# Attention and a dense mixture of experts on one core: the last v scale by TensorE, and the second halves of the weight splits by ScalarE and VectorE

## The chip, the core and the metric

The kernel runs on one core of one Trainium2 chip. The metric is the device time of one execution in microseconds (us). Engine names as in the profile: PE is TensorE's matrix multiplication and PEld its weight load, DVE is VectorE, ACT is ScalarE, POOL is GpSimd, SP is SyncE, which here only issues DMA. L12 is line 12 of the kernel.

## The reference

Causal attention with a decay, for 4 batches of 8 heads (S = 576 positions, D = 64), and behind it a mixture of 4 experts in which every expert runs on every token:

```python
scores = scale * q @ k.T + (cum[i] - cum[j]);  causal mask;  attn = softmax(scores)
x = (attn @ v)  ->  tokens 2304 x 512
p = domain_probs / (domain_probs.sum(-1, keepdims=True) + 1e-09)
for e in range(4):
    h = np.maximum(x @ w1[e], 0.0)          # 512 -> 1024
    out += p[:, e:e + 1] * (h @ w2[e])      # 1024 -> 512
```

Inputs and output are float32.

## The kernel before

**Numbers as pairs.** Most products run in f16 at float32 quality: a number is scaled by a power of two and written as a high part (`hi`, `wh`, `gh`) and the f16 of the rest (`lo`, `wl`, `gl`), and a product is the sum of high times high, high times low and low times high. A split therefore has two steps: ScalarE writes the scaled number as f16, and another engine takes that from the scaled number. The scale of a tensor is a power of two near its largest magnitude, so it needs a maximum over all 128 partitions.

**Order of work.** Attention comes in two halves of the queries (`JOBS`): in the first half the heads' keys are 256 long, in the second up to 576. The expert layers come in groups (an expert's weights in two halves each, `GROUPS`) of four units of 128 x 1024, a unit holding 512 columns of the first layer (`k == 0`) and 512 of the second (`k == 1`). Until about 85 us the start runs, with the first four groups on float32 pairs; from about 85 to 206 us runs what is here called the first sweep, the groups of steps 4 to 7 on the first tokens, while the later heads of the first half of attention are computed; then the heads of the second half with more groups until about 590 us; then a part in which the sums of products are formed in another way, to the end. The program's text gives the steps of heads (`head_steps`, with `bounds[n]` as extra work at head n), and a scheduler puts the instructions of all engines in an order by its own plan of durations. Each engine then carries out its list strictly in that order, and so does SP with the DMAs.

**Weight units.** `w_split` (L1020 to L1056) splits a unit that was loaded as float32 (`wr`, loaded at L989). There are 32 such units: 16 in the first sweep, 8 around 325 to 365 us and 8 around 480 to 545 us. For the first-layer half, ScalarE writes `wh` (L1043) and VectorE `wl` (L1044, `scalar_tensor_tensor`). For the second-layer half, the number is first scaled in place (first sweep: ScalarE, L1033; later: GpSimd, L1035), ScalarE casts it (L1038), and GpSimd subtracts (L1039). L1053 stores some of the pairs in DRAM for later.

**The v scale.** The scale of v for the second half of attention is global over the batch. `v_scale` (L390 to L430) comes in two parts, `top` at `bounds[30]` and `finish` at `bounds[31]`. `top` reduces over the free axis (L401), has SP write the column of 128 maxima to DRAM (L402, tile `dv`) and read it back, broadcast to all partitions (L403, `tops`); `finish` reduces along the free axis (L408) and forms the power of two and its reciprocal (L409 to L421), into column B of `vsc` and `xun`. These are used by the splits of v in the second half of attention (`prep_v`, L572 and L573) and by `weigh` (L442, GpSimd), which makes the factors `scg` of the sums L1142. The other scales (of weights, `topw`; of v per batch, `topx`) go through `power` (L200 to L241), with PE moving the maxima: a transpose (L206), a reduction and three small steps on VectorE (L209 to L220), a tiny matmul with ones that broadcasts (L227), and `finish` on VectorE (L236, L239).

**Who uses what, around it.** L1077 is the first layer (`l` for gate, its weights `wh`, `wl`), ScalarE (L1090, `gh`) and VectorE (L1091, `gl`) make the hidden pair, L1113 is the second layer, and VectorE's L1142 weights the result into `acc` and so frees the PSUM tile for the next chunk's L1113. L638 are the scores, VectorE's L652 adds the mask and finds the maximum `nm`, L749 splits the probabilities (`z`), and SP's L761 transposes them by DMA into `pt`.

Of the kernel before, what the change touches and what calls it, by code (L numbers as in the profile page):

```python
# [8 lines left out]
F32 = mybir.dt.float32  # L9
F32R = mybir.dt.float32r  # L10
F16 = mybir.dt.float16
I32 = mybir.dt.int32  # L12
AF = mybir.ActivationFunctionType
ALU = mybir.AluOpType
AX = mybir.AxisListType

B, H, S, D = 4, 8, 576, 64
E, DM, FF = 4, 512, 1024
NT = B * S
# [18 lines left out]
SWEEP_1 = 8  # L38
# [42 lines left out]
TINY = 2.0**-26  # L81
EXPONENT = 0x7F800000
# [3 lines left out]
def fused(ctx: ExitStack, tc: tile.TileContext, qk, v, f, probs, w, out):  # L86
    nc = tc.nc
# [4 lines left out]
    const = SB("const", 1)  # L92
# [18 lines left out]
    dr_p = ctx.enter_context(tc.tile_pool(name="dr", bufs=4, space=bass.MemoryType.DRAM))  # L111
# [14 lines left out]
    vmax = const.tile([128, 16], F32, name="vmax")  # L126
    vsc = const.tile([128, 8], F32, name="vsc")
    xsc = const.tile([128, 8], F32, name="xsc")
    xun = const.tile([128, 8], F32, name="xun")
    tops = const.tile([128, 256], F32, name="tops")  # L130
    pr_r = tops[:, : NT // 128 * E].rearrange("p (t e) -> p t e", e=E)
    ones_r = const.tile([4, 128], F32, name="ones_r")
    scg = const.tile([128, 8, NT // 128], F32, name="scg")
    sc0 = const.tile([128, 2, E], F32, name="sc0")
# [109 lines left out]
    known = set()  # L244
# [121 lines left out]
    NV = 6  # L366
# [23 lines left out]
    def v_scale():  # L390

        m = vmax[:, NV : NV + 1]
        d = dr_p.tile([128, 1], F32, tag="dv", name="dv", bufs=1)
        u = vmax[:, NV + 1 : NV + 2]

        def top():
            assert all(("x", b) in known for b in range(B))
            nc.vector.tensor_tensor(
                out=vmax[:, :B], in0=vmax[:, :B], in1=xsc[:, :B], op=ALU.max
            )  # L400
            nc.vector.tensor_reduce(out=m, in_=vmax[:, :NV], op=ALU.max, axis=AX.X)  # L401
            nc.sync.dma_start(out=d, in_=m)  # L402
            nc.sync.dma_start(  # L403
                out=tops[:, :128], in_=d.rearrange("q k -> (q k)").partition_broadcast(128)
            )

        def finish():
            nc.vector.tensor_reduce(out=u, in_=tops[:, :128], op=ALU.max, axis=AX.X)  # L408
            nc.vector.tensor_scalar(out=u, in0=u, scalar1=TINY, scalar2=None, op0=ALU.max)  # L409
            nc.vector.tensor_scalar(  # L410
                out=u.bitcast(I32),
                in0=u.bitcast(I32),
                scalar1=EXPONENT,
                scalar2=None,
                op0=ALU.bitwise_and,
            )
            nc.vector.reciprocal(out=vsc[:, B : B + 1], in_=u)
            nc.vector.tensor_scalar(
                out=xun[:, B : B + 1], in0=u, scalar1=2.0**-2, scalar2=None, op0=ALU.mult
            )  # L420
            nc.vector.tensor_scalar(  # L421
                out=vsc[:, B : B + 1],
                in0=vsc[:, B : B + 1],
                scalar1=2.0**14,
                scalar2=None,
                op0=ALU.mult,
            )
            known.add(("x", B))

        return top, finish  # L430

    weighed = set()

# [487 lines left out]
    bounds = {}  # L921
    for b in range(2, B):
        n = 2 * NPR * b
# [5 lines left out]
        bounds[n - 1] = [(100, parts[3])]  # L929

    parts_v = v_scale()
    bounds[30] = [(50, parts_v[0])]
    bounds[31] = [(50, parts_v[1])]

    def head_steps(n):

# [29 lines left out]
    wh, wl, wraw, loaded = {}, {}, {}, {}  # L966
# [50 lines left out]
    def w_fetch(n):  # L1017
        nc.sync.dma_start(out=w_pair(n), in_=wd[unit(n)])

    def w_split(n):  # L1020
        if n not in RAWS:
            w_fetch(n)
            return
        r = wraw.pop(n)
        g = GROUPS[n // 4][0]
        assert ("w", g) in known
        t = w_pair(n)
        for k in range(2):
            c = slice(512 * k, 512 * k + 512)
            sc = wsc[:, g, k : k + 1]  # L1030
            if k == 1:
                if n // 4 < SWEEP_1:
                    nc.scalar.activation(out=r[:, c], in_=r[:, c], func=AF.Copy, scale=sc)  # L1033
                else:
                    nc.gpsimd.tensor_scalar(  # L1035
                        out=r[:, c], in0=r[:, c], scalar1=sc, scalar2=None, op0=ALU.mult
                    )
                nc.scalar.activation(out=wh[n][:, c], in_=r[:, c], func=AF.Copy)  # L1038
                nc.gpsimd.tensor_tensor(  # L1039
                    out=wl[n][:, c], in0=r[:, c], in1=wh[n][:, c], op=ALU.subtract  # L1040
                )
                continue
            nc.scalar.activation(out=wh[n][:, c], in_=r[:, c], func=AF.Copy, scale=sc)  # L1043
            nc.vector.scalar_tensor_tensor(  # L1044
                out=wl[n][:, c],
                in0=r[:, c],
                scalar=sc,
                in1=wh[n][:, c],
                op0=ALU.mult,
                op1=ALU.subtract,  # L1050
            )
        if (g in KEPT) == (n // 4 < SWEEP_1):
            at_step(step + 1, lambda: nc.sync.dma_start(out=wd[unit(n)], in_=t))  # L1053
        i = RAWS.index(n) + RAW
        if i < len(RAWS):
            w_load(RAWS[i])  # L1056
# [779 lines left out]
```

## Time and profile before

| what | us |
|---|---|
| three runs | 934.6, 935.0, 940.25 |
| median | 935.0 |
| the profiled execution | 933.63 |
| its span in the trace | 931.8 |
| PE busy | 866.4 (93%) |
| DVE busy | 712.5 (76%) |
| ACT busy | 544.4 (58%) |
| POOL busy | 463.9 (50%) |
| mean granted clock of PE, share of full speed | 0.989 |

Busy is the time in which an engine carries out instructions; PE at 93% leaves 65 us in the span without a matmul. In a row of the timeline the columns are the start (us), the duration (us), engine, line, operation, output<-input with shape and type, and in square brackets the idle time of the engine before it with what ended it; xN joins N neighbours of one kind. In a row of waits: the waiting engine and line, <- what it waited for, then total us, how often, and the longest us. In a row of instruction groups: line, engine, operation, output<-input, shape, count | busy us, mean ns of one | idle before us and what ended it.

### The profile page before, as it was taken

To read this page: it belongs to the slowest core of one execution; us is meant where nothing else is said; L and a number is where in the kernel's file an instruction comes from. 1 tells how busy PE (TensorE), PEld (TensorE's weight loads), DVE (VectorE), ACT (ScalarE), POOL (GpSimd) and SP (SyncE) were. 2 spreads that over 40 slices of the span, in tenths; PEclk is the share of its full clock that TensorE was granted. 3 is DMA by queue.
4 is the path that set the end of the run, shared out by engine and by line. 5 is a ranking of instruction groups with operands and counts; after the bars stand their busy time and mean duration, and the time that the engine had idled before them with its cause. 6 is when DMAs were issued, how large, how long until landed. Compare 5 with 4: busy or idle time off the path is not lost.

```text
span 931.8 us, 16630 instructions
## 1 busy us (share of the span) xinstructions
PE 866.4 (93%) x5756; PEld 570.8 (61%) x5756; DVE 712.5 (76%) x1496; ACT 544.4 (58%) x1118; POOL 463.9 (50%) x496
## 2 busy tenths in 40 slices
PE   3698989879999998999999899999998999999998
PEld 2577756446667665676766576654455664666547
DVE  5589799836888899878888867655678747786487
ACT  5766849435676685665767765445655345653350
POOL 3746645344325275325238520384778627885060
PEclk9999999989999999999999999999999999999999
DMA  8667889949999999985897984254322422241003
GB/s 281 197 180 235 232 273 250 256 120 270 252 236 258 228 255 276 238 235 125 209 286 228 299 184 76 56 187 140 114 74 91 159 91 89 70 124 36 24 1 91
DMA packets 167236, 163.64 MB, mean 176 GB/s; under 512 B 105108, under 2 KB 129872, under 8 KB 167152
## 3 DMA queue, kind: packets, MB, share of 16 engines
q1 hardware_dynamic: 167152, 162.58, 62.8%
q8 instruction: 45, 0.74, 0.3%
q14 instruction: 39, 0.32, 0.1%
HBM read 116.78 MB, written 21.64 MB: 149 GB/s over the span
## 4 chain that ended last, share of the span: by engine, by line
PE 48%; POOL 9%; DVE 8%; ACT 6%; issue 3%; DMA 1%; SPq 0%; POOLq 0%; ACTq 0%; DVEq 0%
PE l L1077 13%; PE l L1113 13%; PE y L1348 8%; PE m L1348 8%; PE s L638 4%; POOL s L1408 4%; POOL wt L1245 3%; PE o L848 3%; POOL wu L1245 1%; DVE z L749 1%; DVE rl L1234 1%; ACT wt L1272 1%; DVE acc L1142 1%; DVE h L1383 1%; ACT r L1394 1%
## 5 line engine op out<-in xcount | busy, mean ns | idle before, releaser
L1077 PE MATMUL l<-y,w 128*128 128x256 f16 x1728 | 213.9, 274 | 2.1 <-DVE w L1044 2.1
L1077 PEld LDWEIGHTS <-w 128*128 128x128 f16 x1728 | 162.7, 98 | 43.6 <-issue 7.4
L1113 PE MATMUL l<-w,gh 128*128 128x512 f16 x568 | 173.6, 389 | 9.6 <-DVE acc L1142 9.6
L667 ACT ACTIVATE p<-p,nm 128x576 f32<-128x576 f32 (+2 forms) x160 | 95.7, 599 | 87.2 <-DVE nm L652 74.9
L586 POOL CAST q<-raw 64x320 fp32r<-64x320 f32 (+1 forms) x56 | 27.0, 482 | 193.3 <-issue 88.5
L749 DVE SCALAR_TENSOR_TENSOR z<-p,rs,z 128x384 f16<-128x384 f32 (+5 forms) x176 | 109.5, 645 | 16.6 <-ACT z L748 15.3
L1113 PE MATMUL l<-w,gl 128*128 128x512 f16 x284 | 108.4, 387 | 6.9 <-DVE gl L1091 6.9
L748 ACT ACTIVATE z<-p,rs 128x384 f16<-128x384 f32 (+5 forms) x176 | 88.6, 550 | 31.5 <-issue 17.7
L1142 DVE SCALAR_TENSOR_TENSOR acc<-y,scg,acc 128x256 f32<-128x256 f32 (+1 forms) x164 | 81.2, 516 | 14.9 <-PE y L1348 14.7
L1113 PEld LDWEIGHTS <-gh 128*128 128x128 f16 x568 | 51.5, 99 | 60.2 <-issue 19.3
L638 PE MATMUL s<-hi 128*128 128x384 f32 (+1 forms) x192 | 77.1, 409 | 10.9 <-POOL hi L600 5.8
L652 DVE CUSTOM_DVE_ANT_0 p<-s,mask 128x288 f32<-128x288 f32 (+2 forms) x160 | 74.2, 474 | 16.4 <-PE s L638 16.1
L1348 PE MATMUL m<-rh,bs 128*128 128x512 f16 x256 | 86.4, 379 | 0.2 <-POOL bs L1277 0.2
L594 POOL TENSOR_TENSOR kl<-raw,hi 64x576 fp32r<-64x576 f32 (+1 forms) x56 | 66.2, 1182 | 17.8 <-ACT hi L585 17.1
L1277 POOL TENSOR_TENSOR bs<-wt,bs 128x512 f16<-128x512 f32 x32 | 37.9, 1190 | 73.4 <-ACT bs L1276 73.0
L1091 DVE SCALAR_TENSOR_TENSOR gl<-l,gh 128x512 f16<-128x512 f32 (+1 forms) x80 | 54.7, 684 | 16.3 <-ACT gh L1090 15.6
L1348 PE MATMUL m<-rh,bw 128*128 128x512 f16 x191 | 64.5, 379 | 1.0 <-ACT r L1394 0.9
L585 ACT ACTIVATE hi<-raw 128x896 fp32r<-128x896 f32 (+1 forms) x56 | 45.3, 808 | 34.3 <-DMA raw<-in_qk 13.7
L638 PE MATMUL s<-kl,q 66*128 66x384 f32 (+1 forms) x192 | 61.6, 327 | 0.0
L1348 PEld LDWEIGHTS <-bs 128*128 128x128 f16 x384 | 37.5, 98 | 38.8 <-POOL bs L1277 0.7
L1383 DVE SCALAR_TENSOR_TENSOR h<-s,h 128x512 f16<-128x512 f32 x40 | 46.4, 1165 | 17.8 <-ACT h L1382 17.5
L1348 PEld LDWEIGHTS <-h 128*128 128x128 f16 x480 | 46.9, 98 | 14.8 <-issue 2.6
(389 smaller groups left out, 1889.2 us busy)
## 6 DMA issues: line engine op xcount, KB each, us to landing
wr<-in_w SPq DMA_DIRECT2D x74, 512.0 KB
wd<-w SPq DMA_DIRECT2D x32, 512.0 KB
w<-wd SPq DMA_DIRECT2D x32, 512.0 KB
raw<-in_qk SPq DMA_DIRECT2D x32, 448.0 KB
wp<-in_w SPq DMA_DIRECT2D x32, 256.0 KB
bv<-wd SPq DMA_DIRECT2D x32, 256.0 KB
bw<-wd SPq DMA_DIRECT2D x32, 256.0 KB
raw<-in_qk SPq DMA_DIRECT2D x24, 256.0 KB
```

The lines of the kernel that those rows point to most:

```text
L594: eng.tensor_tensor(out=kl[:64, :wk], in0=r[:64, ko : ko + wk], in1=hi[:64, ko : ko + wk].bitcast(F32), op=ALU.subtract,)
L638: nc.tensor.matmul(out=ps[:, at : at + z - a], lhsT=lhsT, rhs=rhs, start=(m == 0), stop=(m == 1),)
L652: nc.vector.tensor_tensor_reduce(out=pt[:, a:z], in0=ps, in1=mask[:, m0 + a : m0 + z], scale=-0.125, scalar=BIG if n == 0 else nm[:, col : ...
L667: nc.scalar.activation(out=pt[:, :w_], in_=pt[:, :w_], func=AF.Exp, scale=-1.0, bias=self.nmax[hh][:, c : c + 1], accum_out=self.ssum[:, h ...
L748: nc.scalar.activation(out=o[:, 0], in_=x, func=AF.Copy, scale=sc)
L749: nc.vector.scalar_tensor_tensor(out=o[:, 1], in0=x, scalar=sc, in1=o[:, 0], op0=ALU.mult, op1=ALU.subtract)
L1077: nc.tensor.matmul(out=self.l1p[:, fi, :], lhsT=lhsT, rhs=rhs[:, k, :], start=(k == 0 and m == 0), stop=(k == 3 and m == 2),)
L1091: self.last = nc.vector.scalar_tensor_tensor(out=self.gl, in0=self.l1p, scalar=0.0, in1=self.gh.bitcast(F32) if wide else self.gh, op0=ALU ...
L1113: matmul(out=l2[tt], lhsT=lhsT, rhs=rhs, start=(opens and fi == 0 and m == 0), stop=(closes and fi == 1 and m == 2),)
L1142: nc.vector.scalar_tensor_tensor(out=acc[c][:, tt, d0:d1], in0=ps, scalar=sc, in1=acc[c][:, tt, d0:d1], op0=ALU.mult, op1=ALU.add,)
L1348: line.append(nc.tensor.matmul(**args))
L1383: nc.vector.scalar_tensor_tensor(out=t[:, 1], in0=x, scalar=0.0 if relu else 1.0, in1=t[:, 0], op0=op, op1=ALU.subtract,)
```

## The change

`v_scale` no longer goes through DRAM. It is built by `power(1, m, "v", use)` and has three parts at `bounds[29]`, `[30]` and `[31]`: free-axis maximum on VectorE and transpose on PE; VectorE's four small steps and the broadcasting matmul; VectorE's `finish` with the two factors. `tops` shrinks to a tile `pr_t` for the probabilities. In `w_split` the branch for `k == 1` is gone: both halves are split by L1043 on ScalarE and L1044 on VectorE.

```diff
-    tops = const.tile([128, 256], F32, name="tops")
-    pr_r = tops[:, : NT // 128 * E].rearrange("p (t e) -> p t e", e=E)
+    pr_t = const.tile([128, NT // 128 * E], F32, name="pr_t")
+    pr_r = pr_t.rearrange("p (t e) -> p t e", e=E)
     def v_scale():
         m = vmax[:, NV : NV + 1]
-        d = dr_p.tile([128, 1], F32, tag="dv", name="dv", bufs=1)
-        u = vmax[:, NV + 1 : NV + 2]
+
+        def use(u, r):
+            nc.vector.tensor_scalar(
+                out=xun[:, B : B + 1], in0=u, scalar1=2.0**-2, scalar2=None, op0=ALU.mult
+            )
+            nc.vector.tensor_scalar(
+                out=vsc[:, B : B + 1], in0=r, scalar1=2.0**14, scalar2=None, op0=ALU.mult
+            )
+            known.add(("x", B))
...
             nc.vector.tensor_reduce(out=m, in_=vmax[:, :NV], op=ALU.max, axis=AX.X)
-            nc.sync.dma_start(out=d, in_=m)
-            nc.sync.dma_start(
-                out=tops[:, :128], in_=d.rearrange("q k -> (q k)").partition_broadcast(128)
-            )
-
-        def finish():
-            nc.vector.tensor_reduce(out=u, in_=tops[:, :128], op=ALU.max, axis=AX.X)
...
-            known.add(("x", B))
-
-        return top, finish
+
+        across, exponent, finish = power(1, m, "v", use)
+        return lambda: (top(), across()), exponent, finish
...
-    bounds[30] = [(50, parts_v[0])]
-    bounds[31] = [(50, parts_v[1])]
+    for n in range(3):
+        bounds[29 + n] = [(50, parts_v[n])]
...
             sc = wsc[:, g, k : k + 1]
-            if k == 1:
-                if n // 4 < SWEEP_1:
-                    nc.scalar.activation(out=r[:, c], in_=r[:, c], func=AF.Copy, scale=sc)
-                else:
-                    nc.gpsimd.tensor_scalar(
-                        out=r[:, c], in0=r[:, c], scalar1=sc, scalar2=None, op0=ALU.mult
-                    )
-                nc.scalar.activation(out=wh[n][:, c], in_=r[:, c], func=AF.Copy)
-                nc.gpsimd.tensor_tensor(
-                    out=wl[n][:, c], in0=r[:, c], in1=wh[n][:, c], op=ALU.subtract
-                )
-                continue
             nc.scalar.activation(out=wh[n][:, c], in_=r[:, c], func=AF.Copy, scale=sc)
             nc.vector.scalar_tensor_tensor(
```

The scheduler plans anew, so the lists of all engines differ from about 85 to 540 us; behind that they are nearly the same. Three places, with the names as above and numbers of tiles behind them (line numbers of the changed kernel are lower: L1013 is what L1044 was, L1022 is L1053, L970 is L989, L742 is L761, L730 is L749, L1060 is L1091, L1111 is L1142).

SP's list before, where the two small DMAs of the v scale stand, in the second half of the first sweep:

```order
L533 DMA raw_1_0_1_2332<-in_qk 128x512
L558 DMA kl_2_0_0_2458<-ncd 2x256
L402 DMA dv<-vmax 128x1
L403 DMA tops<-dv 128x128
L761 DMA_TRANSPOSE pt_0_0_0_2311<-z_691 128x2x128
L761 DMA_TRANSPOSE pt_0_0_0_2311<-z_691 128x4x128
L989 DMA wr_2422<-in_w 128x1024
L989 DMA wr_2430<-in_w 128x1024
L1053 DMA wd_159<-w_2416 128x2048
L1053 DMA wd_160<-w_2424 128x2048
```

SP's list of the changed kernel at the same place, before the same transposes of `pt_0_0_0`:

```order
L970 DMA wr_2410<-in_w 128x1024
L1022 DMA wd_159<-w_2405 128x2048
L970 DMA wr_2417<-in_w 128x1024
L1022 DMA wd_160<-w_2412 128x2048
L970 DMA wr_2521<-in_w 128x1024
L1022 DMA wd_161<-w_2516 128x2048
L970 DMA wr_2528<-in_w 128x1024
L539 DMA kl_2_0_1_2508<-ncd 2x256
L742 DMA_TRANSPOSE pt_0_0_0_2300<-z_692 128x2x128
L742 DMA_TRANSPOSE pt_0_0_0_2300<-z_692 128x4x128
```

The transposes stood behind the DMA that reads `dv` back; now loads and stores of weight units stand there, and no DMA of the v scale.

VectorE's list before, around the reduction L408 of what came back from DRAM:

```order
L702 TENSOR_SCALAR ss_0_0_2239<-ss_0_0_2239 128x2
L705 RECIPROCAL rs_0_0_2240<-ss_0_0_2239 128x2
L749 SCALAR_TENSOR_TENSOR z_691<-p_0_0_0_0_2236,rs_0_0_2240,z_691 128x128
L408 TENSOR_REDUCE vmax<-tops 128x1
L409 TENSOR_SCALAR vmax<-vmax 128x1
L410 TENSOR_SCALAR vmax<-vmax 128x1
L749 SCALAR_TENSOR_TENSOR z_691<-p_0_0_0_1_2237,rs_0_0_2240,z_691 128x2x128
L417 RECIPROCAL vsc<-vmax 128x1
L418 TENSOR_SCALAR xun<-vmax 128x1
L421 TENSOR_SCALAR vsc<-vsc 128x1
L1142 SCALAR_TENSOR_TENSOR acc_1097<-l_6_6_0_0_0_2381,scg,acc_1097 128x512
L1142 SCALAR_TENSOR_TENSOR acc_1097<-l_6_6_0_0_1_2388,scg,acc_1097 128x512
```

VectorE's list of the changed kernel at the same place (its L408 is the free-axis maximum, L401 before):

```order
L683 TENSOR_SCALAR ss_0_0_2228<-ss_0_0_2228 128x2
L408 TENSOR_REDUCE vmax<-vmax 128x1
L1013 SCALAR_TENSOR_TENSOR w_2405<-wr_1666,wsc,w_2405 128x512
L1013 SCALAR_TENSOR_TENSOR w_2412<-wr_1673,wsc,w_2412 128x512
L686 RECIPROCAL rs_0_0_2229<-ss_0_0_2228 128x2
L1013 SCALAR_TENSOR_TENSOR w_2405<-wr_1666,wsc,w_2405 128x512
L1013 SCALAR_TENSOR_TENSOR w_2412<-wr_1673,wsc,w_2412 128x512
L1013 SCALAR_TENSOR_TENSOR w_2516<-wr_1778,wsc,w_2516 128x512 x2
L1013 SCALAR_TENSOR_TENSOR w_2523<-wr_1785,wsc,w_2523 128x512
L1111 SCALAR_TENSOR_TENSOR acc_1098<-l_6_6_0_0_0_2370,scg,acc_1098 128x512
L1013 SCALAR_TENSOR_TENSOR w_2523<-wr_1785,wsc,w_2523 128x512
L1060 SCALAR_TENSOR_TENSOR gl_6_1_0_2473<-l_6_6_1_0_2422,gh_6_1_0_2472 128x512
```

Ahead of the first `acc` of that chunk stood the reduction that waits for the DMA; now seven splits of weights stand there, an eighth between it and the next `gl`.

VectorE's list of the changed kernel some 50 rows later, where the maxima come back from PE's transpose (`topv`; `uv` is a small tile in SBUF):

```order
L209 TENSOR_REDUCE uv<-topv 1x1
L210 TENSOR_SCALAR uv<-uv 1x1
L213 TENSOR_SCALAR uv<-uv 1x1
L883 SCALAR_TENSOR_TENSOR y_2591<-o_0_0_2578,y_2591 128x256
L220 TENSOR_SCALAR uv<-ident,uv 1x1
L554 SCALAR_TENSOR_TENSOR v_2_0_2615<-vh_1539,vsc,v_2_0_2615 128x4x64
L683 TENSOR_SCALAR ss_2_0_2613<-ss_2_0_2613 128x2
L686 RECIPROCAL rs_2_0_2614<-ss_2_0_2613 128x2
```

Between the four steps of the exponent and their neighbours stands other work; `finish` follows ten rows later (L236, L239 and the two factors in a row).

## Rows read from the trace of the kernel before

**Rows 1.** The page, busy time of the engines (us, share of the span, instructions).
```profile
PE 866.4 (93%) x5756; PEld 570.8 (61%) x5756; DVE 712.5 (76%) x1496; ACT 544.4 (58%) x1118; POOL 463.9 (50%) x496
```
**Rows 2.** Waits of PE over the run.
```profile
PE l L1113 <- DVE acc L1142: 9.6, 4, 6.1
PE l L1113 <- DVE gl L1091: 8.4, 8, 2.3
PE s L638 <- DVE nm L652: 4.5, 2, 4.1
PE topx L227 <- DVE ux L220: 3.7, 3, 1.9
```
**Rows 3.** Timeline, 186 to 202 us, all engines.
```profile
186.32 0.69 DVE L1091 SCALAR_TENSOR_TENSOR gl<-l,gh 128x512 f16<-128x512 f32 x1 [0.28 <-ACT gh L1090]
186.88 0.34 SPq L402 DMA_DIRECT2D dv<-vmax  x1
...
188.48 1.03 PE L1113 MATMUL l<-w,gh 128*128 128x512 f16 x4
...
191.07 2.35 PE L1077 MATMUL l<-y,w 128*128 128x256 f16 x20
...
193.81 0.32 SPq L403 DMA_DIRECT2D tops<-dv  x1
...
194.22 6.40 SPq L761 DMA_TRANSPOSE pt<-z  x2
198.35 0.29 DVE L408 TENSOR_REDUCE vmax<-tops 128x1 f32<-128x128 f32 x1 [10.38 <-DMA tops<-dv]
...
200.40 1.87 PE L1113 MATMUL l<-w,gh 128*128 128x512 f16 x4 [6.07 <-DVE acc L1142]
```
**Rows 4.** Busy time by stretch: us, PE, PEld, DVE, ACT, POOL, clock, DMA share, GB/s.
```profile
118.00:172.00 54.00, 46.27 (x320) 29.65 (x318) 53.90 (x129) 34.34 (x84) 28.79 (x40) 0.97 0.90 266
...
195.00:200.00 5.00, 0.00 (x0) 0.00 (x0) 1.58 (x8) 0.00 (x0) 0.29 (x1) 0.90 0.31 26
200.00:205.00 5.00, 3.82 (x9) 1.12 (x9) 4.30 (x13) 1.47 (x5) 5.00 (x10) 0.50 0.73 166
...
340.00:360.00 20.00, 18.29 (x140) 12.48 (x137) 18.98 (x32) 14.07 (x27) 19.69 (x16) 1.00 0.90 262
```
**Rows 5.** The broadcasting matmuls of `power`, instruction groups of PE, whole run.
```profile
L227 PE MATMUL topw<-uw,ones_r 2*128 2x2 f32 x16 | 3.0, 256 | 0.6 <-DVE uw L220 0.6
```
**Rows 6.** Instructions of L1044: count, shortest, median, longest (ns), first and last start.
```profile
L1044 DVE SCALAR_TENSOR_TENSOR w<-wr,wsc,w x32: 730/750/1951, 106.5 to 526.2; 128x512 f16<-128x512 f32 x32
```
**Rows 7.** Timeline, GpSimd's subtractions and VectorE beside them, first sweep.
```profile
161.04 2.26 POOL L1039 TENSOR_TENSOR w<-wr,w 128x512 f16<-128x512 f32 x2
161.28 2.04 DVE L702 TENSOR_SCALAR ss<-ss 128x2 f32<-128x2 f32 x1
```
**Rows 8.** Instruction groups of DVE by shape, 85 to 206 us.
```profile
L1044 DVE SCALAR_TENSOR_TENSOR w<-wr,wsc,w 128x512 f16<-128x512 f32 x16 | 12.7, 811 | 1.8 <-POOL scg L442 1.0 <-ACT w L1043 0.8
...
L749 DVE SCALAR_TENSOR_TENSOR z<-p,rs,z 128x128 f16<-128x128 f32 x14 | 9.2, 660 | 0.0
```
**Rows 9.** The same, 206 to 280 us, where no unit is split.
```profile
L749 DVE SCALAR_TENSOR_TENSOR z<-p,rs,z 128x128 f16<-128x128 f32 x6 | 2.1, 346 | 0.5 <-ACT z L748 0.5
```
**Rows 10.** Instruction groups of DVE, 325 to 365 us.
```profile
L1044 DVE SCALAR_TENSOR_TENSOR w<-wr,wsc,w 128x512 f16<-128x512 f32 x8 | 8.2, 1031 | 0.0
```
**Rows 11.** Timeline of VectorE, four splits of probabilities at two times.
```profile
354.99 5.59 DVE L749 SCALAR_TENSOR_TENSOR z<-p,rs,z 128x384 f16<-128x384 f32 x4
...
510.13 2.26 DVE L749 SCALAR_TENSOR_TENSOR z<-p,rs,z 128x384 f16<-128x384 f32 x4
```
**Rows 12.** Instruction groups of DVE by shape, 480 to 545 us.
```profile
L1044 DVE SCALAR_TENSOR_TENSOR w<-wr,wsc,w 128x512 f16<-128x512 f32 x8 | 10.8, 1363 | 0.0
```
**Rows 13.** Instruction groups of ACT, 85 to 545 us, splits of weights.
```profile
L1043 ACT ACTIVATE w<-wr,wsc 128x512 f16<-128x512 f32 x32 | 22.5, 711 | 1.8 <-PE s L638 1.2 <-DVE wsc L341 0.4
...
L1038 ACT ACTIVATE w<-wr 128x512 f16<-128x512 f32 x32 | 19.4, 616 | 0.0
```

More of the change, by code (lines that the diff above doesn't have):

```diff
@@ L401, in top @@
             nc.vector.tensor_reduce(out=m, in_=vmax[:, :NV], op=ALU.max, axis=AX.X)
-            nc.sync.dma_start(out=d, in_=m)
-            nc.sync.dma_start(
-                out=tops[:, :128], in_=d.rearrange("q k -> (q k)").partition_broadcast(128)
-            )
-        def finish():
-            nc.vector.tensor_reduce(out=u, in_=tops[:, :128], op=ALU.max, axis=AX.X)
[L409 to L415, printed above, removed]
-            )
-            nc.vector.reciprocal(out=vsc[:, B : B + 1], in_=u)
-            nc.vector.tensor_scalar(
-                out=xun[:, B : B + 1], in0=u, scalar1=2.0**-2, scalar2=None, op0=ALU.mult
-            )
[L421 to L427, printed above, removed]
-            known.add(("x", B))
-        return top, finish
+        across, exponent, finish = power(1, m, "v", use)
+        return lambda: (top(), across()), exponent, finish
     weighed = set()
@@ L1030, in w_split @@
             sc = wsc[:, g, k : k + 1]
-            if k == 1:
-                if n // 4 < SWEEP_1:
-                    nc.scalar.activation(out=r[:, c], in_=r[:, c], func=AF.Copy, scale=sc)
-                else:
-                    nc.gpsimd.tensor_scalar(
-                        out=r[:, c], in0=r[:, c], scalar1=sc, scalar2=None, op0=ALU.mult
-                    )
-                nc.scalar.activation(out=wh[n][:, c], in_=r[:, c], func=AF.Copy)
-                nc.gpsimd.tensor_tensor(
-                    out=wl[n][:, c], in0=r[:, c], in1=wh[n][:, c], op=ALU.subtract
-                )
-                continue
             nc.scalar.activation(out=wh[n][:, c], in_=r[:, c], func=AF.Copy, scale=sc)
```

## The prediction

> **What bounds the kernel now.** I read the page's busy times first: PE works for 866.4 of 931.8 us [rows 1], so a change that adds no work to PE can only win from the 65 us in which PE stands still, and from stretches at a lower clock. Next, the waits of PE: which of them does the change touch? Four rows matter [rows 2]. The longest single wait, 6.1 us, is for an `acc` of VectorE, and VectorE's list shows what it stood behind: the reduction L408, which waits for the v scale to come back from DRAM.
>
> The timeline of that place tells the whole story [rows 3]. SP issues the write of `dv` at 186.88 and can issue the read only at 193.81, 6.9 us later; VectorE, strictly in order, sits idle for 10.38 us until 198.35; SP's transposes of `z` stand behind the read and start at 194.22. PE runs out of work and idles 6.07 us until 200.40. The windows show the end of it [rows 4]: from 195 to 200 us PE, PEld and ACT do nothing, and from 200 to 205 us PE's granted clock is 0.50, the lower of its two levels (1.2 instead of 2.4 GHz), after that idle stretch. This is the one place where everything stops.
>
> The second question is how full VectorE is where it gets new work. From 118 to 172 us it is busy 53.90 of 54 us, from 340 to 360 us 18.98 of 20 with GpSimd at 19.69 [rows 4]. There VectorE, not PE, sets the pace.
>
> **The change part by part.**
>
> *The v scale.* Both DMAs go, and with them VectorE's wait, so PE's 6.07 us are open to be won. Of the stretch at 0.50, PE's 3.82 us of work [rows 4] would take half at full clock: 1.9 us. What comes in: two small operations on PE, a transpose and the broadcasting matmul. `power` already runs such matmuls at 256 ns [rows 5]; with the transpose taken alike, 0.5 us. VectorE's small steps are about as many as before (eight there, nine now), and I cost them at nothing since they stood on VectorE before. PE's L227 waits for VectorE's L220. The trace of before has that wait for `topx`: 3.7 us in three, the longest 1.9 [rows 2], so its bounds are 0 and 1.9. In the changed order about 35 PE instructions stand between transpose and matmul and VectorE has ready work between, so I take 0.5. Queued behind L227 on PE are the first-layer products of the next group; no other engine waits for `vsc` and `xun` until the second half's v and the factors of the next chunks, some ten rows later on VectorE. SP's ten rows around no longer hold a wait for a DMA; the transposes now stand behind loads and stores of weight units, which wait for VectorE's last split.
>
> *What is late next.* The first `acc` of that chunk now stands behind seven splits, and the next `gl` behind eight. One split takes 0.750 us at the median [rows 6]. From one `gl` to the next VectorE has: eight splits, 6.0; one `acc`, about 0.75 (the size of a split, PSUM on one side); one `gl`, 0.69 [rows 3]; two pieces of `z`, the smaller 0.35 [rows 9], together about 0.8; four small steps with the reduction at 0.29 or less [rows 3], about 0.7. That is 8.9 us. PE has, from the order, 12 second-layer matmuls of 0.26 (four took 1.03), 24 first-layer matmuls of 0.117 (twenty took 2.35) [rows 3], two more of the second layer and six for scores that I put at the 0.256 of [rows 5]: 3.1 + 2.8 + 0.5 + 1.5 = 7.9 us. So of the 6.07 us about 1.0 comes back as a wait for the splits; its bounds are 0 (VectorE arrives early) and 6.07 (the hole only changes its cause).
>
> *The splits.* VectorE gets 32 operations of 0.750 us, 24.0 us: 12.0 in the first sweep and 6.0 in each of the two later stretches. GpSimd loses 32 subtractions and 16 scalings. ScalarE's 32 casts of 0.616 become scaled casts of 0.711 [rows 13], +3.0 us, and 16 scalings on it vanish; ScalarE wins a little and I cost it at nothing.
>
> VectorE gets part of the 24.0 us back. Where GpSimd subtracts, VectorE's operations on SBUF are stretched: at 161.28 a 128x2 `tensor_scalar` takes 2.04 us, from just after the start of two L1039 to their end [rows 7]. One shape of `z` split takes 0.660 us in the first sweep [rows 8] and 0.346 us where no unit is split [rows 9]: 14 x 0.314 = 4.4. L1044 itself has 0.811 in the first sweep: 16 x 0.061 = 1.0. With 1.9 for the L702 of [rows 7], 7.3 of the 12.0 us come back. From 325 to 365 us: L1044 at 1.031 [rows 10], 8 x 0.281 = 2.2, and four `z` splits in 5.59 us that take 2.26 us elsewhere [rows 11], 3.3; together 5.5 of 6.0. From 480 to 545 us: L1044 at 1.363 [rows 12], 8 x 0.613 = 4.9 of 6.0. Over the run VectorE grows by 24.0 - 17.7 = 6.3 us.
>
> What of this reaches PE? In the first sweep the net 4.7 us are covered by the 10.38 us in which VectorE stood idle, beside the bunch already counted: 0. From 325 to 365 us the four stretched `z` splits stand just ahead of the wait of 4.1 us for `nm` [rows 2]; GpSimd's other subtractions, for the heads, stay, so I take half: -2.0. From 480 to 545 us the net 1.1 us count in full. Together -0.9. The bounds: every such wait goes (below, -11.8), or nothing comes back (+18).
>
> A page of the Trainium skill states a stronger rule: in "SBUF — State Buffer", section "SBUF: two separate sides", VectorE with two SBUF inputs and a GpSimd operation that reads SBUF take one shared port pair as an exclusive lock for the whole instruction, and the loser blocks fully. The stretched rows agree in kind [rows 7], and the longest L1044 of 1.951 against 0.730 us [rows 6] is one subtraction of 1.13 (half of the pair's 2.26) more, less a tenth. By that rule all 32 subtractions could stop VectorE, an estimate of 36 us by the row's 1.13, more than the 24.0 added, and VectorE would end up freer than before; the counted stretching, 17.7 us, says less.
>
> *The sum.* -6.07 - 1.9 + 0.5 + 0.5 + 1.0 - 0.9 = -6.9 us. The profiled execution took 933.6 us and lies 1.4 below the median of 935.0; so 926.8 on its basis, 928.1 on the median's, which I forecast.
>
> **The rivals.**
>
> *The stalls behind stretched operations go too.* What the change takes off GpSimd would then be worth more than the hole. The remaining waits of PE for `acc` are 9.6 - 6.1 = 3.5, for `nm` 4.1, for `gl` half of 8.4, 4.2 [rows 2]: 11.8 us, in place of my -0.9: about 917 us. For it: [rows 7, 11] show the stretching where VectorE is full. Against it: each stretch gets 6 to 12 us of new operations on the same engine. The port rule named above would have it come out this way.
>
> *VectorE becomes the bound, on the other side.* In the full stretches [rows 4] every split that is not paid for by less stretching delays `gl`, `acc` and `nm`, and PE with them. If nothing comes back, the 16 of the first sweep and the 8 around 350 us cost 18 us, and 928.1 + 0.9 + 18 = 947 us. The sum without the splits is -6.0, so it decides as soon as more than 6.0 us of the added 24.0 reach PE: then the kernel is slower than before. For it: 53.90 of 54. Against: the stretched rows, and VectorE's idle 10.38 us. Another page argues this way: the Trainium skill, "Perfetto Trace Analysis", section "Optimizing Scalar/DVE Operations", has work taken off a saturated VectorE, to ScalarE or even GpSimd, the reverse of this change, but adds that a move to GpSimd may not help because they share a port; the trace bears out the second half [rows 7].
>
> *The hole only moves.* The chain transpose, four steps, matmul, `finish` spans 20 rows of VectorE's list and holds one of the score tiles' PSUM buffers; PE's L227 may wait its 1.9 us, and the bunch of splits its whole bound. Then the 7.9 us shrink to 2 or 3: about 933 us.
>
> **How the numbers follow.** The forecast (hole gone, splits about even; own range 923 to 934) 0.50; stalls gone too, 917, 0.25; the hole moves, 933, 0.14; VectorE the bound, 937 to 947, 0.11. One per cent, about what a measurement here can tell from no change, is 9.35 us: faster means below 925.6, slower above 944.4. Faster takes the second case whole and 0.15 of the first, 0.40. Slower takes 0.08 of the fourth; the rest is within 1%, 0.52. For 8 in 10 the range reaches well into the second case and to the near end of the fourth: 915 to 938.
>
> **What would show it.** Right: no idle VectorE of 10 us near 190 to 200 us, a clock near 1.00 there, L1044 with 64 instances near 0.75 and no longest of 1.9, the `z` splits of 128x128 near 0.35 in the first sweep, a wait of about 1 us for the `gl` or `acc` behind the bunch. Wrong: PE waits on L227 of `topv` for several us; PE's sums of waits for `acc` and `gl` in the first sweep above the 3.5 and 8.4 of now; or L749 still at 0.66 with GpSimd's splits gone, which would mean that the heads' subtractions stretch it, not those of the weights.

## The result, and the profile after

The changed kernel takes 913.4 us (median of 4, 911.9 to 915.8), the kernel before 935.6 beside it. The ratio is 0.976, with a 95% interval of 0.973 to 0.979: 22 us faster, where 928.1 was forecast (-6.9) and 915 to 938 was the range. The case that came closest is the rival "the stalls behind stretched operations go too", 917 us.

The page of the changed kernel, busy times, answers to [rows 1]:

```profile
span 910.2 us, 16597 instructions
...
PE 860.8 (95%) x5759; PEld 573.1 (63%) x5759; DVE 712.4 (78%) x1530; ACT 538.5 (59%) x1102; POOL 398.9 (44%) x448
```

Two things are to be seen. VectorE got 32 more splits, 24.0 us by the prediction's price, and its busy time is the same, 712.5 before and 712.4 now. And PE's account closes: its busy time fell by 5.6 us (866.4 to 860.8), its time without a matmul from 65.4 to 49.4 us, by 16.0; together the 21.6 us by which the span is shorter.

PE's waits over the run, after, in the columns of [rows 2]:

```profile
PE topx L227 <- DVE ux L220: 4.9, 2, 3.0
PE l L1082 <- DVE gl L1060: 3.7, 2, 2.6
...
PE l L1082 <- DVE acc L1111: 2.0, 3, 1.2
...
PE s L619 <- DVE nm L633: 0.9, 1, 0.9
```

Waits for `acc` fell from 9.6 to 2.0, for `gl` from 8.4 to 3.7, for `nm` from 4.5 to 0.9: 15.9 us, about as much as PE's idle time lost (smaller rows, up and down, about cancel). Only 6.1 of them were the hole of the v scale. There is no wait of L227 for the new `uv`; the row for `topx` belongs to earlier chains.

The splits and their neighbours on VectorE, instruction groups by shape of the changed kernel, 85 to 194 us (the first sweep), columns as in [rows 8]:

```profile
L1013 DVE SCALAR_TENSOR_TENSOR w<-wr,wsc,w 128x512 f16<-128x512 f32 x32 | 23.3, 770 | 0.9 <-ACT w L1012 0.8
...
L730 DVE SCALAR_TENSOR_TENSOR z<-p,rs,z 128x128 f16<-128x128 f32 x14 | 6.2, 441 | 0.0
```

The same, 311 to 347 us and 460 to 524 us, where the later units are split:

```profile
L1013 DVE SCALAR_TENSOR_TENSOR w<-wr,wsc,w 128x512 f16<-128x512 f32 x16 | 11.7, 754 | 0.0
```

```profile
L1013 DVE SCALAR_TENSOR_TENSOR w<-wr,wsc,w 128x512 f16<-128x512 f32 x16 | 13.6, 884 | 0.0
```

A split took 0.811, 1.031 and 1.363 us in these stretches [rows 8, 10, 12] and takes 0.770, 0.754 and 0.884 now; in the middle stretch 16 splits take 11.7 us where 8 took 8.2. Not every stretched one is gone: the longest split still takes 1.893 us, where "no longest of 1.9" was to be a sign of being right, and the `z` splits of 128x128 take 0.441 us, between the 0.660 of before and the 0.346 that was expected. The bunch of splits ahead of `acc` is where the order put it, in VectorE's timeline of the changed kernel:

```profile
183.19 1.40 DVE L1013 SCALAR_TENSOR_TENSOR w<-wr,wsc,w 128x512 f16<-128x512 f32 x2
...
184.59 3.38 DVE L1013 SCALAR_TENSOR_TENSOR w<-wr,wsc,w 128x512 f16<-128x512 f32 x5
187.88 0.74 DVE L1111 SCALAR_TENSOR_TENSOR acc<-l,scg,acc 128x512 f32<-128x512 f32 x1
188.55 0.74 DVE L1013 SCALAR_TENSOR_TENSOR w<-wr,wsc,w 128x512 f16<-128x512 f32 x1
189.21 0.68 DVE L1060 SCALAR_TENSOR_TENSOR gl<-l,gh 128x512 f16<-128x512 f32 x1
```

No wait of PE goes with it. A run of splits costs 0.68 apiece from start to start (3.38 for five), less than the 0.750 of one alone, and PE's only wait from 172 to 200 us is 2.63 us at 180.62, for the `gl` ahead of the bunch. The busy times by stretch say the same, in the columns of [rows 4]:

```profile
118.00:172.00 54.00, 51.30 (x372) 34.61 (x371) 51.72 (x138) 28.38 (x71) 18.41 (x31) 1.00 0.85 252
172.00:206.00 34.00, 31.31 (x232) 21.39 (x231) 29.12 (x80) 22.89 (x58) 11.79 (x17) 1.00 0.98 314
```

From 118 to 172 us PE works 51.30 us where it worked 46.27, and VectorE is less full than before (51.72 of 54, against 53.90), with more operations (138 against 129). The mean granted clock of PE is 1.00 in both stretches, against 0.97 and 0.90 before.

### The profile page after: what moved, and what is told of

Its sections match the earlier page's. It is cut to its first block, busy times and chain, and to the rows that moved or that the text cites. A ratio compares the mean times of both kernels' runs of the same rounds, so it can differ in the third digit from the quotient of the medians.

```text
span 910.2 us, 16597 instructions
## 1 busy us (share of the span) xinstructions
PE 860.8 (95%) x5759; PEld 573.1 (63%) x5759; DVE 712.4 (78%) x1530; ACT 538.5 (59%) x1102; POOL 398.9 (44%) x448
## 4 chain that ended last, share of the span: by engine, by line
PE 56%; DVE 15%; POOL 12%; ACT 7%; DMA 5%; issue 5%; SPq 1%; POOLq 0%; DVEq 0%; ACTq 0%
PE l L1082 17%; PE l L1046 17%; PE y L1317 6%; PE m L1317 6%; PE s L619 5%; POOL s L1377 5%; POOL wt L1214 4%; PE o L829 3%; DMA wr<-in_w 2%; POOL wu L1214 2%; DVE w L1013 2%; DVE wl L986 1%; DVE acc L1111 1%; ACT wt L1241 1%; DVE rl L1203 1%
## 5 line engine op out<-in xcount | busy, mean ns | idle before, releaser
L1082 PE MATMUL l<-w,gh 128*128 128x512 f16 x568 | 169.1, 380 | 2.2 <-DVE acc L1111 2.0
L567 POOL CAST q<-raw 64x320 fp32r<-64x320 f32 (+1 forms) x56 | 29.5, 526 | 250.1 <-issue 134.3
L648 ACT ACTIVATE p<-p,nm 128x576 f32<-128x576 f32 (+3 forms) x160 | 95.6, 598 | 52.6 <-DVE nm L633 42.8
L1082 PE MATMUL l<-w,gl 128*128 128x512 f16 x284 | 105.8, 379 | 3.8 <-DVE gl L1060 3.7
L730 DVE SCALAR_TENSOR_TENSOR z<-p,rs,z 128x384 f16<-128x384 f32 (+5 forms) x176 | 96.9, 577 | 14.3 <-ACT z L729 13.1
L729 ACT ACTIVATE z<-p,rs 128x384 f16<-128x384 f32 (+5 forms) x176 | 88.8, 550 | 25.5 <-DVE rs L686 6.5
L1111 DVE SCALAR_TENSOR_TENSOR acc<-y,scg,acc 128x256 f32<-128x256 f32 (+1 forms) x164 | 81.1, 515 | 14.9 <-PE y L1317 14.7
L1060 DVE SCALAR_TENSOR_TENSOR gl<-l,gh 128x512 f16<-128x512 f32 (+1 forms) x80 | 54.7, 684 | 12.4 <-ACT gh L1059 11.5
L1059 ACT ACTIVATE gh<-l 128x512 f16<-128x512 f32 (+1 forms) x80 | 46.9, 586 | 25.5 <-PE l L1046 25.1
```

Of the source, the lines that this page charges most:

```text
L648: nc.scalar.activation(out=pt[:, :w_], in_=pt[:, :w_], func=AF.Exp, scale=-1.0, bias=self.nmax[hh][:, c : c + 1], accum_out=self.ssum[:, h ...
L729: nc.scalar.activation(out=o[:, 0], in_=x, func=AF.Copy, scale=sc)
L730: nc.vector.scalar_tensor_tensor(out=o[:, 1], in0=x, scalar=sc, in1=o[:, 0], op0=ALU.mult, op1=ALU.subtract)
L1060: self.last = nc.vector.scalar_tensor_tensor(out=self.gl, in0=self.l1p, scalar=0.0, in1=self.gh.bitcast(F32) if wide else self.gh, op0=ALU ...
L1082: matmul(out=l2[tt], lhsT=lhsT, rhs=rhs, start=(opens and fi == 0 and m == 0), stop=(closes and fi == 1 and m == 2),)
L1111: nc.vector.scalar_tensor_tensor(out=acc[c][:, tt, d0:d1], in0=ps, scalar=sc, in1=acc[c][:, tt, d0:d1], op0=ALU.mult, op1=ALU.add,)
```

## The experiments

### Which part gave what: four kernels with one part each

**vscale_only** has the new `v_scale` and the old branch for `k == 1`; **splits_only** the reverse.

```diff
 vscale_only: the changed kernel, w_split as before the change
+            if k == 1:
+                ...  (L1031 to L1042 of the kernel before)
+                continue
 splits_only: the kernel before, without that branch
```

> The v scale by TensorE alone; all weight units are split as before, with GpSimd. Theory A (the change gave 22 us, of which the hole at 190 to 200 us is 7 to 8 and the rest is VectorE freed from GpSimd's subtractions): 926 to 929 us, and the other waits for acc, gl and nm stay. Theory B (the hole cost more than its idle time, since work piled up behind it; the 16 us gained in the first sweep are all the v scale's): 918 to 921 us.

Measured: 928.9 us against 935.3 (ratio 0.993, 0.991 to 0.995).

> Both halves of all 32 units split by ScalarE and VectorE; the v scale still goes through DRAM. Theory A: 919 to 922 us, the hole of about 10 us on VectorE stays. Theory B: 926 to 929 us, only the two later stretches win, 5 and 3.5 us.

Measured: 921.6 us against 935.3 (0.984, 0.980 to 0.988).

**first_sweep** has the new `v_scale` and takes the old branch only for the later units; **later_units** only for the first sweep.

```diff
 first_sweep
+            if k == 1 and n // 4 >= SWEEP_1:
 later_units
+            if k == 1 and n // 4 < SWEEP_1:
```

> The v scale by TensorE, and the 16 units of the first sweep split by ScalarE and VectorE; the 16 later units as before. Both theories: about 921 us, since the marks of the later stretches lie 5 and 3.5 us apart in the changed kernel and stay so here (-22 + 8.5 = -13.5).

Measured: 919.0 us (0.983, 0.980 to 0.986).

> The v scale by TensorE, and only the 16 later units split by ScalarE and VectorE; the first sweep as before. Theory A: -7.5 for the hole and -8.5 for the later stretches, about 919 us, and VectorE full from 118 to 172 us as before. Theory B: about 913 us, as the changed kernel.

Measured: 919.6 us (0.983, 0.980 to 0.987).

Three of the four tell theory A from theory B, and all three come out as theory A has it; first_sweep was expected alike by both. The v scale alone gives 6.4 us, the splits alone 13.7; the sum, 20.1, is a little under the 22.2 of both. On top of the v scale (928.9 us), the splits of the first sweep give 6.2 to 9.9 us and the later ones 5.6 to 9.3, each by which of the two is added first (919.0, 919.6 and 913.4 us). Where the time goes is read by marks: the start of the same `gl` of VectorE in the six profiled executions, as time in the kernel before and difference to it in us:

| mark (before) | vscale_only | splits_only | first_sweep | later_units | changed |
|---|---|---|---|---|---|
| 102.0 | +0.8 | +1.8 | +0.1 | +0.8 | +1.7 |
| 168.0 | +1.6 | -9.6 | -11.5 | +2.8 | -9.8 |
| 202.3 | -5.2 | -12.5 | -14.7 | -3.9 | -13.1 |
| 280.8 | -4.5 | -6.5 | -15.0 | -4.3 | -13.4 |
| 406.2 | -6.0 | -11.8 | -15.0 | -9.9 | -18.7 |
| 573.1 | -6.0 | -12.2 | -15.0 | -13.0 | -22.2 |

At 168 us the kernels with the first sweep's splits on VectorE are some 10 us ahead, before the v scale's hole. A mark is one instruction, though, and its place in the order counts too: at the `gl` that starts at 157.7 us before, splits_only stands at -3.3 and the changed kernel at -3.0, at the one of 176.0 us at +4.1 and +3.9. Surer is that PE works 50.35 us from 118 to 172 us in splits_only, where it worked 46.27 before:

```profile
118.00:172.00 54.00, 50.35 (x366) 33.84 (x366) 51.38 (x136) 28.16 (x70) 18.39 (x31) 1.00 0.86 251
```

And from 280 us on first_sweep is 9 to 10.5 us ahead of vscale_only. The later stretches give about 5 us near 325 to 400 and 3.5 near 480 to 570. The old splits left their mark on PE in vscale_only, timeline and waits:

```profile
167.24 1.93 PE L1094 MATMUL l<-w,gh 128*128 128x512 f16 x4 [3.86 <-DVE acc L1123]
```

```profile
PE l L1094 <- DVE gl L1072: 7.1, 7, 2.3
...
PE s L619 <- DVE nm L633: 4.1, 1, 4.1
PE l L1094 <- DVE acc L1123: 4.1, 2, 3.9
```

In splits_only the wins shrink from 12.5 to 6.5 us between 202 and 281 us. There the new plan sets other work between the two DMAs and moves the reduction of `tops` back, so VectorE waits only 1.78 us for it. As the trace reads, the round trip is paid by SP and by what follows it, SP's waits (165 to 215 us), SP's timeline, and PE's waits over the run:

```profile
SPq L558 <- DMA dv<-vmax: 6.0, 1, 6.0
```

```profile
198.17 6.89 SPq L761 DMA_TRANSPOSE pt<-z  x4
...
207.40 0.41 SPq L403 DMA_DIRECT2D tops<-dv  x1
```

```profile
PE o L848 <- DMA pt<-z: 7.8, 5, 3.0
```

A small DMA of keys' decay waits 6.0 us in SP's list at the place of the round trip, four transposes are late, and PE waits for `pt`: 7.8 us over the run, where it waited 1.0 before, and 3.6 of them from 202 to 285 us, where the win shrinks. The windows of that stretch, splits_only and then first_sweep, show a lower clock besides:

```profile
206.00:280.00 74.00, 70.43 (x505) 47.87 (x505) 59.52 (x159) 46.44 (x105) 26.34 (x39) 0.98 0.96 231
```

```profile
206.00:280.00 74.00, 74.00 (x553) 50.90 (x551) 62.45 (x158) 47.56 (x105) 32.27 (x41) 1.00 0.98 231
```

With the v scale on PE no DMA of it stands there: that is a part of the change which the splits alone don't give.

### Why freeing GpSimd helps: its operations beside VectorE

**pool_two_inputs** and **pool_one_input** are the changed kernel with useless work for GpSimd at the places where it used to subtract, written to a scratch tile (`idle`) that nobody reads.

```diff
+            if k == 1:
+                for o in (0, 128):
 pool_two_inputs
+                    nc.gpsimd.tensor_tensor(out=idle, in0=mask[:, o : o + 384],
+                        in1=wh[n][:, 512 + o : 896 + o], op=ALU.subtract)
 pool_one_input
+                    nc.gpsimd.tensor_scalar(out=idle, in0=wh[n][:, 512 + o : 896 + o],
+                        scalar1=0.5, scalar2=None, op0=ALU.mult)
```

> The changed kernel, and for each of the 32 units GpSimd also does two subtractions of 128x384 (from a mask tile and the unit's high part, both in SBUF) into a scratch tile that nobody reads. No engine waits for them but a buffer that comes free, so only their running beside VectorE can cost time. Theory A (GpSimd's reads of SBUF hold up VectorE's operations on SBUF): 922 to 928 us, L1044's successor well above 0.75 us at the mean, z splits of 128x128 in the first sweep near 0.6 us again. Theory C (what was won is the shorter chain ScalarE, GpSimd, TensorE and another order): 913 to 915 us.

Measured: 942.2 us, beside 913.4 for the changed kernel on the same chip (**after_again**): +28.8, far more than the 922 to 928 us that theory A had expected.

> The same with GpSimd operations of one SBUF input (a scaling of the unit's high part, 128x384). Theory A, if any GpSimd access to SBUF holds VectorE up: as with two inputs, in proportion to the time that GpSimd spends. If only two-input subtractions do: 913 to 915 us, and the split's mean stays at 0.76.

Measured: 913.8 us: +0.4.

> The changed kernel on the same chip as the three others: 912 to 915 us. In the profiled execution the granted clock was 0.50 from 35 to 60 us; if that belongs to the kernel it is there again, if to the single execution it is not.

Measured: 913.4 us (909.2 to 915.0), with a granted clock of 1.00 from 40 to 60 us.

The instruction groups of the useless work, pool_two_inputs and then pool_one_input:

```profile
L1016 POOL TENSOR_TENSOR idle<-mask,w 128x384 f16<-128x384 f32 x64 | 70.9, 1108 | 21.4 <-ACT w L1013 18.0
```

```profile
L1016 POOL TENSOR_SCALAR idle<-w 128x384 f16<-128x384 f16 x64 | 81.5, 1274 | 15.5 <-ACT w L1013 11.5
```

and VectorE beside each, groups by shape from 85 to 560 us: splits (two inputs in SBUF), `gl` (one input in PSUM), and a reduction (one input in SBUF), first with pool_two_inputs, then with pool_one_input, last the splits of the changed kernel alone:

```profile
L1019 DVE SCALAR_TENSOR_TENSOR w<-wr,wsc,w 128x512 f16<-128x512 f32 x64 | 70.1, 1130 | 0.8 <-ACT w L1013 0.8
L1066 DVE SCALAR_TENSOR_TENSOR gl<-l,gh 128x512 f16<-128x512 f32 x61 | 41.7, 683 | 5.4 <-ACT gh L1065 5.0
...
L320 DVE TENSOR_REDUCE wmax<-wp 128x1 f32<-128x512 f32 x32 | 21.6, 675 | 0.0
```

```profile
L1019 DVE SCALAR_TENSOR_TENSOR w<-wr,wsc,w 128x512 f16<-128x512 f32 x64 | 52.7, 858 | 0.8 <-ACT w L1013 0.8
L1066 DVE SCALAR_TENSOR_TENSOR gl<-l,gh 128x512 f16<-128x512 f32 x65 | 44.4, 684 | 6.1 <-ACT gh L1065 5.5
...
L320 DVE TENSOR_REDUCE wmax<-wp 128x1 f32<-128x512 f32 x32 | 21.6, 676 | 0.0
```

```profile
L1013 DVE SCALAR_TENSOR_TENSOR w<-wr,wsc,w 128x512 f16<-128x512 f32 x64 | 48.5, 794 | 0.9 <-ACT w L1012 0.8
```

GpSimd works longer in the second kernel, 81.5 against 70.9 us, and costs nothing, while 70.9 us of two-input subtractions cost 28.8. A split takes 1.130 us at the mean with them, 0.858 with the scalings and 0.794 with neither; `gl` and the reduction don't feel either. VectorE's busy time is 745.0 us with the one, 717.3 with the other and 711.4 in after_again. So GpSimd subtracting two SBUF operands costs, and VectorE pays where it combines two SBUF operands. A `tensor_scalar` with a single tensor, in SBUF, pays as well: in pool_two_inputs one of 128x2 lasts just to the end of the subtraction beside it, 0.87 us, where one with GpSimd idle takes 0.15:

```profile
152.15 1.24 POOL L1016 TENSOR_TENSOR idle<-mask,w 128x384 f16<-128x384 f32 x1
152.54 0.87 DVE L684 TENSOR_SCALAR ss<-ss 128x2 f32<-128x2 f32 x1
```

The page "SBUF — State Buffer" of the Trainium skill, section "SBUF: two separate sides", gives the lock for a VectorE operation with two SBUF inputs, but against any GpSimd operation that reads SBUF; for one-input GpSimd work of f16 this case measures 0.858 against 0.794 us for a split and no effect on the time, and the measurement decides. The two kernels differ in type too: the useless subtraction reads f32 and f16, the scaling f16 alone. GpSimd's scaling in the kernel before is f32 of 128x512, and such a one does hold VectorE up, for a part of its time. In sub_on_dve (below) a `tensor_scalar` of 128x3 takes 0.68 us beside one of 1.56 us, where 0.17 is its median:

```profile
474.69 1.56 POOL L1016 TENSOR_SCALAR wr<-wr,wsc 128x512 f32<-128x512 f32 x1
474.71 0.68 DVE L683 TENSOR_SCALAR ss<-ss 128x3 f32<-128x3 f32 x1 [0.94 <-ACT p L648]
```

Useless f32 scalings were not tried.

### What VectorE's own time costs

**dve_extra** is the changed kernel with two more subtractions of 128x256 per unit on VectorE.

```diff
+            if k == 1:
+                for o in (0, 256):
+                    nc.vector.tensor_tensor(out=idle[:, :256], in0=mask[:, o : o + 256],
+                        in1=wh[n][:, 512 + o : 768 + o], op=ALU.subtract)
```

> The changed kernel, and for each unit VectorE does two more subtractions of 128x256 into a scratch tile that nobody reads, about 26 us of VectorE in all, with nothing more on GpSimd. This prices VectorE's own time, and with it what the moved subtractions cost. If VectorE's time is what PE waits for where units are split: +10 to +15 us in the first sweep and +3 to +6 later, 927 to 934 us. If VectorE had room for them: 913 to 918 us.

Measured: 926.8 us (925.4 to 931.7), 13.5 above the changed kernel, at the near end of what was expected if VectorE's time counts. Busy times of its profile:

```profile
PE 864.2 (93%) x5759; PEld 571.7 (62%) x5759; DVE 739.0 (80%) x1594; ACT 537.8 (58%) x1102; POOL 403.9 (44%) x448
```

VectorE's 27.6 us more (739.0 against 711.4) cost 13.5 us, about half. So the new splits are not free. By the same half the change pays about 12 of its 24.0 us there, an estimate, and then gets 27.5 us back from what GpSimd no longer does: 12 and the 15.5 won on top of the v scale. That this is near the 28.8 of the useless subtractions shows nothing, since those fill 70.9 us of GpSimd and the subtractions taken away 40.7 (L1039 before; its scalings, L1035, 25.5). The next section has the subtraction alone.

### Subtraction, scaling or chain

**sub_on_dve** keeps scaling and cast as before and moves only the subtraction to VectorE; **sub_scalar** besides has ScalarE scale the later units as well.

```diff
 sub_on_dve, in the branch k == 1
-                nc.gpsimd.tensor_tensor(
+                nc.vector.tensor_tensor(
                     out=wl[n][:, c], in0=r[:, c], in1=wh[n][:, c], op=ALU.subtract
 sub_scalar, besides
-                if n // 4 < SWEEP_1:
-                    nc.scalar.activation(out=r[:, c], in_=r[:, c], func=AF.Copy, scale=sc)
-                else:
-                    nc.gpsimd.tensor_scalar(
-                        out=r[:, c], in0=r[:, c], scalar1=sc, scalar2=None, op0=ALU.mult
-                    )
+                nc.scalar.activation(out=r[:, c], in_=r[:, c], func=AF.Copy, scale=sc)
```

> The v scale by TensorE; the second halves are scaled and cast as before the change (ScalarE, and GpSimd's one-input scaling in the 16 later units), and only the subtraction goes to VectorE, as a tensor_tensor of two SBUF inputs. If the two-input subtractions on GpSimd are the whole cause (Theory A as the runs have sharpened it): 912 to 917 us, like the changed kernel, with L1035's successor still on GpSimd. If GpSimd's scalings hold VectorE up as well, or ScalarE's saved passes count: 919 to 924 us.

Measured: 920.5 us (916.9 to 922.2; the kernel before took 934.4 to 935.8 at the median beside the runs compared here). The subtraction alone gives 8.4 of the 15.5 us between vscale_only and the changed kernel, so it is not the whole cause. With half of the 21.7 us that 32 subtractions of 0.679 us add to VectorE, taking GpSimd's away was worth about 19 us; the price of the useless ones, 28.8 us for 70.9 of GpSimd, gives 16.5 for their 40.7. Both are estimates, and they are of one size.

> As sub_on_dve (only the subtraction moved to VectorE), but the 16 later units are scaled in place by ScalarE like those of the first sweep, so GpSimd has no part in any split of a unit. If GpSimd's one-input scaling makes up the 7 us between sub_on_dve (920.5) and the changed kernel (913.4): 913 to 916 us. If it is the longer chain of three steps for a half instead of two: 918 to 922 us.

Measured: 915.5 us (913.1 to 919.0). Without GpSimd's scaling most of the rest seems to come, too, but the two kernels' times overlap, so the 5 us between their medians are not shown. By the marks, in one execution of each, it is in the two later stretches that sub_on_dve falls back (from +1 at 320 us to +7 at 535 us against after_again) and sub_scalar hardly does (+3 and +4). What the longer chain costs, 2 us by the medians, is within the scatter, too. If the scaling costs 5 us, why stays open: it holds some operations of VectorE up for a part of its time, as the rows of sub_on_dve above show, and ScalarE's cast has to wait for it, in GpSimd's list. Neither was tested apart.

### A version that is faster than both

If two-input work of GpSimd beside VectorE is dear, the low parts of the first groups (`w_wide`, units 0 to 15, in turn by VectorE and GpSimd) are the next place.

```diff
-W_DVE = tuple(range(0, 16, 2))
 wide_dve
+W_DVE = tuple(range(16))
 wide_8
+W_DVE = tuple(range(8)) + (8, 10, 12, 14)
 wide_12
+W_DVE = tuple(range(12)) + (12, 14)
```

> The changed kernel, and the low parts of the first four groups' units all by VectorE (1.0 us a piece), none by GpSimd (2.0 us a piece). Theory A alone would have it faster, by up to 8 us, since GpSimd's 16 pieces stand beside VectorE; VectorE is busy 5.00 of 5 us in most windows from 60 to 100 us, though, so if its own time decides there, 16 us more work give 4 to 10 us more: 917 to 924 us.

Measured: 917.7 us, but 914.6 to 922.5, so 1 to 9 us above the changed kernel.

> A version that may beat both: the low parts of units 0 to 7 of the first groups all by VectorE, units 8 to 15 in turn by VectorE and GpSimd as now. With all 16 on VectorE the marks before 105 us came 6 us earlier and those at 120 to 140 us 4 to 14 us later, when VectorE was full. If the early gain stays: 908 to 911 us; if it is eaten as with all 16: 914 to 918 us.

Measured: 907.3 us (0.970 of before, 0.966 to 0.973), 6 us better than the changed kernel.

> The same with units 0 to 11 on VectorE and 12 to 15 in turn. If the early gain stays: 907 to 911 us; if eaten: 914 to 918 us.

Measured: 911.9 us (0.973, 0.970 to 0.977), within the scatter of the changed kernel.

The windows show what the first eight units gain, wide_8 and then after_again (columns as in [rows 4]):

```profile
40.00:60.00 20.00, 17.09 (x82) 15.14 (x83) 16.72 (x48) 13.49 (x36) 4.30 (x7) 1.00 0.66 199
60.00:85.00 25.00, 25.00 (x165) 21.68 (x164) 25.00 (x58) 20.33 (x45) 15.49 (x19) 1.00 0.70 206
85.00:118.00 33.00, 30.58 (x205) 24.23 (x205) 32.23 (x73) 19.51 (x44) 13.96 (x16) 1.00 1.01 287
```

```profile
40.00:60.00 20.00, 16.54 (x74) 14.18 (x74) 13.21 (x40) 12.36 (x33) 12.48 (x15) 1.00 0.53 175
60.00:85.00 25.00, 24.63 (x163) 21.22 (x162) 24.96 (x47) 17.00 (x36) 14.82 (x14) 1.00 0.66 190
85.00:118.00 33.00, 29.91 (x198) 25.06 (x197) 30.16 (x79) 22.13 (x50) 18.71 (x21) 0.95 0.87 240
```

From 40 to 60 us VectorE has room (13.21 of 20) and takes the work from GpSimd, and PE works 17.09 us instead of 16.54. From 60 to 85 us VectorE is full in both, and the low parts that GpSimd keeps in wide_8 start at 72.0 us: moving those as well adds to a full engine. That this is why the other two are slower is not shown, since in wide_12 VectorE works only 26.61 of 33 us from 85 to 118 us.

## Why the prediction was wrong

**The hole of the v scale: right, in part by luck.** The sum without the splits was -6.0 us, or -7.0 without the 1.0 for a bunch of splits that vscale_only does not have; vscale_only gave -6.4. The terms did not come out one by one: in its profile PE's idle time is 7.1 us shorter (65.4 to 58.3), and its busy time 1.8 longer (868.2), with a clock of 0.94 from 118 to 172 us and 0.95 from 172 to 206, so the 1.9 us of clock were not won there. In the changed kernel the chain from PE's transpose at 204.73 to the last factor at 210.22 us takes 5.5 us, and nobody waits: neither the 0.5 us for L227 nor the 1.0 us for the bunch of splits came. Both were small terms on the cautious side, and PE's granted clock there, from 195 to 205 us, is 1.00. The rival "the hole only moves" fell with the changed kernel, though splits_only, where the round trip stays, shows that such a move is real.

**The splits: the step that failed.** The prediction took -0.9 us for them in all, 0 in the first sweep and -0.9 in the two later stretches; they gave 15.5 on top of the v scale and 13.7 alone, 6.2 to 9.9 in the first sweep and 5.6 to 9.3 later. The step is the passage "What of this reaches PE?", with the 17.7 us of stretching that it starts from, and three errors are seen in it.

First, the stretching was counted on a few shapes, 17.7 us; VectorE's unchanged busy time says that about all of the 24.0 came back. (About, since the order alone moves this figure: vscale_only, with the old splits, has 717.5.)

Second, it was set off as time against time, and only the difference was passed on to PE. But a late `acc`, `gl` or `nm` can stop PE at one moment, like the 4.1 us for `nm` behind four stretched `z` splits [rows 2, 11], while time added elsewhere is partly absorbed: dve_extra shows that half of such time reaches the run's. The waits for `gl`, `nm` and `acc` beside the hole fell by 4.7, 3.6 and 1.5 us, 9.8 in all, where the prediction took 2.0 for `nm` and nothing for the others. Its rival with 11.8 had that size about right.

Third, the clock. The prediction counted 1.9 us for the lower level, at the hole alone; PE's busy time fell by 5.6. Before, the mean granted clock was 0.97 from 118 to 172 us [rows 4], 0.90 from 172 to 206 and 0.97 in each of the two later stretches of splits; in the changed kernel it is 1.00 in the stretches at their places. So the waits that went took a time at the lower level with them. This is read from the windows and not tested apart. Over its whole run the profiled execution of the changed kernel has a lower mean clock than the one of before, 0.981 against 0.989, since it stands at 0.50 from 40 to 60 us; after_again, with 1.00 there and 0.998 over the run, has nearly the same busy time of PE, 860.1.

**VectorE as the bound.** Its premise was right and its sign wrong. VectorE sets the pace there, and time added to it costs, about half of it (dve_extra). But 53.90 busy of 54 us [rows 4] was not fullness with work: part of it was VectorE held up inside its instructions, which a profile shows as busy. That reading, "VectorE is full, so the new work can hardly be absorbed", is what kept the rival with the stalls gone at 0.25.

**What the trace had shown.** The row of a 128x2 operation of 2.04 us beside two subtractions [rows 7] showed it held up to the end of the second; the prediction took it as one lump of 1.9 us rather than as the mechanism of the whole stretch. Not all of the win is shown to be this mechanism: the subtraction alone gave 8.4 of the 15.5 us, and how the rest divides between the scaling, the longer chain and the order is open.

## What to carry to other kernels

An engine whose instructions are held up by another looks busy: compare the duration of one shape in a stretch with and without the other engine before calling it full. When such hold-ups lie on an engine that others wait for, price the change by the waits that follow the stretched operations, and by the clock behind each wait, not by the net of busy times. Of the work tried here for GpSimd, VectorE hardly felt f16 operations with one input; two-input ones it paid for.

## What the runs showed of the hardware

- GpSimd's subtractions of two SBUF operands stretched VectorE's splits (two SBUF operands) from 0.794 us at the mean (changed kernel, 85 to 560 us) to 1.130 (pool_two_inputs); its one-input f16 scalings only to 0.858 (pool_one_input). VectorE's `gl`, with one operand in PSUM, stayed at 0.683 and 0.684, reductions of one SBUF operand at 0.675 and 0.676.
- A `tensor_scalar` of one small SBUF tensor was held up as well: 0.87 us to the end of a two-input subtraction (pool_two_inputs), 0.68 us beside a one-input f32 scaling of 1.56 us (sub_on_dve), where 0.15 to 0.17 is usual.
- The same kernel on two executions: the granted clock was 0.50 from 40 to 60 us in the profile first taken of the changed kernel, and 1.00 in after_again, whose span is 2.7 us shorter (907.5 against 910.2).

```profile
40.00:60.00 20.00, 15.68 (x63) 13.48 (x64) 12.93 (x38) 13.17 (x35) 13.52 (x15) 0.50 0.54 174
```

In that stretch PE works 15.68 of 20 us at the lower level, and 16.54 at the higher one, so a stretch with gaps can stand at either; what decides it the runs don't show.
